# Attention with a soft mixture of experts on one core: filler products in two waits of TensorE, and SyncE's written order kept for eight more weight loads

## The chip, the cores and the metric

The kernel runs on one core of a Trainium2 chip. The metric is the device time of one execution in microseconds, the median of several runs. The profile is one further execution, recorded by the hardware.

## The reference

The first half is attention for 8 batches and 8 heads over 576 positions of width 64: queries and keys are rotated by position, the scores go through a softmax, and the result multiplies the values. The second half sends all 4608 rows of the attention output (512 wide) through a soft mixture of 8 experts with 4 slots each.

```python
q_rot, k_rot = rotate(q), rotate(k)
scores = scale * q_rot @ k_rot.T ; attn = softmax(scores) ; x = attn @ v      # rows: 4608 x 512
logits = x @ phi                                                              # 4608 x 32
d = exp(logits - logits.max(0)) ; d /= d.sum(0)
slot_input = (d.T @ x).reshape(8, 4, 512)
slot_out[e] = relu(slot_input[e] @ w1[e]) @ w2[e]                             # w1 512x1024, w2 1024x512
c = softmax(logits, axis=1) ; out = c @ slot_out
```

## The kernel before

**Attention.** Two heads make a pair, and there are 32 pairs (`NPAIR`), 0 to 31. A pair's products run in units: `m` units find the row maxima of the scores, which ScalarE turns into a small tile `mr` (`m_half`) and SyncE copies by two small DMAs into the rows of a tile `peak` (`m_rows`, lines 340 and 341). The `t` units (line 355, and 368 to 370 for the remainder) form the scores again in three half-precision products and subtract the maxima by a fourth product of `lift` and `peak`; ScalarE takes the exponential (line 358). The `av` units (lines 411 and 422) multiply by the values. Then come `norm`, `natural` (transposes, line 325), `natural_out` (ScalarE copies to `xt`, line 474), `logits` (lines 481 and 484) and `logits_sum`.

**Order.** Three tables of due times, `FIRST`, `WHEN` and `LAST`, sort all steps of all pairs into one list. `tc.manual_schedule` makes an engine issue in the order in which the code is written. For TensorE, ScalarE and VectorE that holds in the whole kernel. For SyncE and GpSimd it holds only while the stack `steady` is open; once it is closed, the framework's scheduler chooses where these two engines' later instructions go, and may put a load ahead of instructions that the code wrote earlier.

**Weights.** The expert weights are 64 tiles of 128x1024 floats (512 KB each), 0 to 31 for the first product and 32 to 63 for the second. Thirty are loaded during attention. The next ones go to room that the last pairs free, and all of them are issued by SyncE from line 612:

- `release_io` (once the last pair's queries and keys are split) opens five buffers `wx`, and `release_stk` opens `wk` (for tile 6), `wh1` and `wh0`. These eight loads are not written at that place but appended to the list `later`, which `trickle` empties.
- `release_fore` opens five buffers `wq` and writes their five loads at once.
- `release_att` opens four buffers `wl` and writes four loads.

The due times put every `trickle` step ahead of `release_io`, so the list is emptied by the loop `while later: trickle(p)` behind the last pair. By the order of the calls, `wq` holds tiles 26 to 30, `wx` 31 and 37 to 40, `wk` 6, `wh1` 41, `wh0` 42, and `wl` 43 to 46.

**Behind the last pair.** `natural`, `logits` and their sum for pair 31, the last statistics (`m_run`), and a chain of small products (lines 821 to 865) that ends in the slot inputs `slot_t`. `spend(n, t)` issues n products of the constant tile `lift` with itself, whose result nobody reads; `SPEND` says how many at each of five places. Then the first expert product runs in four parts `ffn1` (line 889), each with 16 tiles' worth of operands: the first part uses tiles 0 to 7. `ffn2_steps` (line 910) is the second product, in four quarters, and `combine` (line 938) forms the output, copied out by ScalarE and VectorE (line 939) into six buffers and written by 18 DMAs of 512 KB (line 941). Seventeen further loads (tiles 47 to 63) take the buffers that the first product frees. `seg_in` (line 875) is a small load between the two groups of loads.

Of the kernel before, what the change touches and what calls it, by code (L numbers as in the profile page):

```python
# [18 lines left out]
NPAIR = B * NP  # L19
# [22 lines left out]
STAGE = (("wx", 5),) * 5 + (("wh0", 1),)  # L42
LEAD_STEPS = 6
N_SLOT = 1
SPEND = (0, 4, 2, 0, 6)
STEPS = (0, 0, 5, 0, 0, 5, 0, 0, 0)
N_WARM = 17
N_HEAT = 12
# [128 lines left out]
def attn_softmoe(ctx, tc, qk, q0, v, phi, w, cs, ident, sel, seg, out):  # L177
    nc = tc.nc
    P = 128
# [24 lines left out]
    steady = ctx.enter_context(ExitStack())  # L204
# [11 lines left out]
    lift = const.tile([P, P], F16, name="lift")  # L216
# [66 lines left out]
    def bank2():  # L283
        turn_of[0] = (turn_of[0] + 1) % 3
        return slots[turn_of[0]].tile([P, 2, 512], F32, name="s_ps")
# [36 lines left out]
    flat = {}  # L322
# [120 lines left out]
    def recip(p):  # L443
        if p not in ons:
            ons[p] = blocks(o_flat[:, O_AT:O_AT + 2 * NJ * VC])
        rrs[p] = rr = small.tile([P, 2 * NJ, 1], F32, name="rr", bufs=2)
        nc.vector.reciprocal(out=rr, in_=ons[p][:, :, D:VC])  # L447
# [28 lines left out]
    def logits(p):  # L476
        xt = xts.pop(p)
        xj = xt[:, 0:512].rearrange("p (h j x) -> p j h x", h=2, j=4)
        flat["l", p] = lp = bank2()[:, 0]
        for j in range(4):  # L480
            nc.tensor.matmul(lp[32 * j:32 * j + 32, 0:P], lhsT=phi_sb[:, p % NP, :], rhs=xj[:, j],
                             start=True, stop=True, tile_position=(0, 32 * j))
        for j in range(4):
            nc.tensor.matmul(lp[32 * j:32 * j + 32, P:192], lhsT=phi_sb[:, p % NP, :], rhs=xt[:, 512:S],  # L484
                             start=True, stop=True, tile_position=(0, 32 * j))
# [123 lines left out]
    def load_w(pool, bufs, tag="w_exp", n=None):  # L609
        n = order.pop(0) if n is None else n  # L610
        wt = pool.tile([P, 2, 512] if n < 4 * E else [P, 4, 256], F32, name=tag, bufs=bufs)
        nc.sync.dma_start(out=wt, in_=w[n].rearrange("p (c f) -> p c f", c=2 if n < 4 * E else 4))
        w_tiles[n] = wt
# [6 lines left out]
    def grow(name, bufs):  # L620
        hold[name] = ctx.enter_context(tc.tile_pool(name=name, bufs=bufs, side="right", reuse_waits="tile"))
        return hold[name]
# [6 lines left out]
    def trickle(p):  # L629
        if later:  # L630
            name, bufs, n = later.pop(0)
            load_w(hold[name], bufs, n=n)
# [10 lines left out]
    def release_att():  # L643
        trans.close()
        grow("wl", N_WL)
        for _ in range(N_WL):
            load_w(hold["wl"], N_WL)
# [20 lines left out]
    def first_rows(p):  # L668
# [26 lines left out]
        "natural": but_last(natural),  # L695
        "natural_out": but_last(natural_out),
        "logits": but_last(logits),
        "logits_sum": but_last(logits_sum),
        "trickle0": trickle, "trickle1": trickle, "trickle2": trickle, "trickle3": trickle,
# [73 lines left out]
        if "wq" not in hold and not held and all(x in done for x in FORE):  # L773
            release_fore()
    p = NPAIR - 1
    steady.close()
    ac, vc = nc.scalar.copy, nc.vector.tensor_copy
    while later:
        trickle(p)
    release_att()  # L780
    recip(p)
    norm(p, nc.vector, True)
# [2 lines left out]
    c_tr(0)  # L785
    natural_out(p)
    logits(p)
    logits_sum(p)
    stat = stat_tasks(B - 1)
# [26 lines left out]
    def spend(n, t):  # L816
        for _ in range(n):
            nc.tensor.matmul(t[:, 256:384], lhsT=lift, rhs=lift, start=True, stop=True)

    spend(SPEND[0], sp)  # L820
    nc.tensor.transpose(mt[:, 0:P], m.broadcast_to([P, P]), id_sb)
    spend(SPEND[1], sp)
    nc.tensor.transpose(tm[:, 0:P], dt[:, 0:P], id_sb)
    spend(SPEND[2], sp)
    nc.tensor.transpose(tr[:, 0:P], dt[:, D:192], id_sb)
    spend(SPEND[3], sp)
    nc.vector.tensor_copy(out=dn[:, 0:P], in_=tm[:, 0:P])
# [18 lines left out]
    for i in range(NP):  # L846
        nc.tensor.matmul(rp[32 * i:32 * i + 32], lhsT=dn[rows[1], P + 32 * i:P + 32 * i + 32],
                         rhs=xn[i][rows[1], 4], start=True, stop=True, tile_position=(64, 32 * i))
# [18 lines left out]
    nc.vector.reciprocal(out=zw, in_=zw)  # L867
    spend(SPEND[4], mt)
    left.close()
# [169 lines left out]
```

## Time and profile before

| | |
|---|---|
| median of 3 runs | 506.17 us |
| lowest and highest | 503.56 and 509.76 us |
| the profiled execution | 507.91 us |
| its span, first to last instruction | 506.1 us |
| mean granted TensorE clock | 0.990 |
| TensorE busy | 478.3 us, 95% |
| VectorE, ScalarE, GpSimd busy | 72%, 57%, 52% |

The span is what the views below show; the profiled execution took a little longer than its span and than the median. A view of waits tells how long an engine stood idle and what ended that. A view of windows gives busy times, the granted clock and the rate of the DMA engines in stretches of the span.

### The profile page before, as it was taken

To read this page: it belongs to the slowest core of one execution; us is meant where nothing else is said; L and a number is where in the kernel's file an instruction comes from. 1 tells how busy PE (TensorE), PEld (TensorE's weight loads), DVE (VectorE), ACT (ScalarE), POOL (GpSimd) and SP (SyncE) were. 2 spreads that over 40 slices of the span, in tenths; PEclk is the share of its full clock that TensorE was granted. 3 is DMA by queue.
4 is the path that set the end of the run, shared out by engine and by line. 5 is a ranking of instruction groups with operands and counts; after the bars stand their busy time and mean duration, and the time that the engine had idled before them with its cause. 6 is when DMAs were issued, how large, how long until landed. Compare 5 with 4: busy or idle time off the path is not lost. (4 is left out here: it accounts for less than half of the span.)

```text
span 506.1 us, 24787 instructions
## 1 busy us (share of the span) xinstructions
PE 478.3 (95%) x11269; PEld 377.9 (75%) x11269; DVE 362.5 (72%) x497; ACT 290.6 (57%) x522; POOL 265.4 (52%) x330
## 2 busy tenths in 40 slices
PE   4799999999999999999999989999999999899993
PEld 2577778878887888788778867887787886753872
DVE  5879879887788788777788668868887761236453
ACT  2355565675657666766676565765566555424442
POOL 3496697945954576458536845576657201120000
PEclk9999999999999999999999999999999999979998
DMA  7325553343544355434544444355335537579888
GB/s 265 127 96 184 212 188 126 122 166 122 206 164 166 122 191 180 157 126 168 204 123 141 136 179 146 125 190 182 128 139 167 187 100 296 199 272 408 330 349 334
DMA packets 27721, 93.96 MB, mean 186 GB/s; under 512 B 4064, under 2 KB 4320, under 8 KB 27616
## 3 DMA queue, kind: packets, MB, share of 16 engines
q1 hardware_dynamic: 27328, 91.79, 50.5%
q8 instruction: 88, 1.44, 1.1%
q10 hardware_dynamic: 288, 0.59, 0.3%
q14 instruction: 17, 0.14, 0.1%
HBM read 82.85 MB, written 9.44 MB: 182 GB/s over the span
## 5 line engine op out<-in xcount | busy, mean ns | idle before, releaser
L253 POOL TENSOR_TENSOR x_in<-x_in,cs_sb 128x288 f32<-128x288 f32 x248 | 206.1, 869 | 106.7 <-DMA x_in<-in_qk 76.0
L303 DVE TENSOR_REDUCE segs<-s_ps 128x14 f32<-128x896 f32 (+1 forms) x160 | 173.6, 1113 | 52.9 <-PE s_ps L300 48.4
L411 PEld LDWEIGHTS o_ps<-v_in,a_t 128*64 128x64 f32 x4608 | 147.1, 137 | 18.4 <-issue 16.6
L411 PE MATMUL o_ps<-v_in,a_t 128*64 128x65 f32 x4608 | 159.2, 224 | 0.9 <-issue 0.6
L358 ACT ACTIVATE a_t<-s_ps 128x896 f32<-128x896 f32 (+1 forms) x160 | 139.5, 943 | 23.3 <-PE s_ps L355 21.1
L355 PE MATMUL s_ps<-hl 64*128 64x448 f16 (+5 forms) x1536 | 121.6, 283 | 0.9 <-DVE segs L303 0.7
L355 PEld LDWEIGHTS <-hl 64*128 64x128 f16 x1536 | 71.8, 94 | 24.5 <-issue 2.0
L451 POOL TENSOR_TENSOR xn<-o_sb,rr 128x512 f32<-128x512 f32 x31 | 33.3, 1075 | 61.3 <-DVE rr L447 47.8
L355 PE MATMUL s_ps<-peak,lift 64*128 64x128 f16 (+5 forms) x512 | 59.3, 283 | 1.2 <-DMA peak<-mr 1.2
L300 PE MATMUL s_ps<-hl 64*128 64x448 f16 (+5 forms) x512 | 56.4, 286 | 0.6 <-DVE segs L303 0.5
L373 ACT ACTIVATE a_rem<-s_ps 128x640 f32<-128x640 f32 x32 | 22.8, 713 | 54.4 <-PE s_ps L370 54.4
L262 ACT CAST hl<-x_in 128x576 f16<-128x576 f32 x62 | 40.6, 673 | 17.0 <-DVE x_in L257 16.9
L270 DVE TENSOR_TENSOR hl<-x_in,hl 128x1152 f16<-128x1152 f32 x32 | 47.6, 1488 | 1.4 <-ACT hl L262 1.3
L257 DVE TENSOR_TENSOR x_in<-x_in 128x1152 f32<-128x1152 f32 x31 | 46.4, 1497 | 2.7 <-POOL x_in L253 2.7
L474 ACT COPY xt<-s_ps 128x576 f32<-128x576 f32 x32 | 20.4, 637 | 43.6 <-PE s_ps L325 43.6
L355 PEld LDWEIGHTS <-lift 64*128 64x128 f16 x512 | 25.9, 94 | 9.8 <-DMA peak<-mr 1.6
L422 PE MATMUL o_ps<-v_in,a_rem 64*64 64x65 f32 x1152 | 29.3, 223 | 3.0 <-issue 2.9
L300 PEld LDWEIGHTS <-hl 64*128 64x128 f16 x512 | 23.7, 95 | 8.8 <-issue 1.9
L315 DVE TENSOR_REDUCE segs<-s_ps 128x2 f32<-128x576 f32 x32 | 24.1, 754 | 7.7 <-PE s_ps L313 7.4
L422 PEld LDWEIGHTS o_ps<-v_in,a_rem 64*64 64x64 f32 x1152 | 25.2, 134 | 4.7 <-issue 4.6
L437 ACT COPY o_sb<-o_ps 128x585 f32<-128x585 f32 x31 | 20.2, 653 | 10.8 <-PE o_ps L422 5.3
L493 DVE TENSOR_TENSOR l_sb<-s_ps,l_sb 128x192 f32<-128x192 f32 x24 | 8.6, 357 | 22.4 <-PE s_ps L484 22.4
(156 smaller groups left out, 536.2 us busy)
## 6 DMA issues: line engine op xcount, KB each, us to landing
x_in<-in_qk SPq DMA_DIRECT2D x62, 576.0 KB
w_exp<-in_w SPq DMA_DIRECT2D x64, 512.0 KB
v_in<-in_v SPq DMA_DIRECT2D x32, 325.0 KB
out<-w_exp SPq DMA_DIRECT2D x18, 512.0 KB
x_in<-in_q SPq DMA_DIRECT2D x4, 288.0 KB
cs_sb<-in_cs ACTq DMA_DIRECT2D x2, 288.0 KB
peak<-mr SPq DMA_DIRECT2D x32, 2.0 KB
peak<-mr SPq DMA_DIRECT2D x32, 0.2 KB
```

The source lines that it names most:

```text
L253: eng.tensor_tensor(out=x[:, :, c], in0=x[:, :, c], in1=cs_sb[:, h, :, at:at + c.stop - c.start], op=ALU.mult)
L257: nc.vector.tensor_tensor(out=x[:, :, 0], in0=x[:, :, 0], in1=x[:, :, 1], op=ALU.add)
L262: nc.scalar.copy(out=halves[p][:, 1 + t], in_=loaded[p][:, t, 0])
L270: nc.vector.tensor_tensor(out=o, in0=x, in1=i, op=ALU.subtract)
L300: nc.tensor.matmul(s[:, h, at], lhsT=hl[rows[h], QH, P * j:P * j + P], rhs=hl[rows[h], KH, cols], start=True, stop=True)
L303: nc.vector.tensor_reduce(out=segs[p % 2][:, 0:8 * SG].rearrange("p (h c) -> p h c", h=2)[:, :, at:at + n // D], in_=s[:, :, 0:n].rearrang ...
L315: nc.vector.tensor_reduce(out=segs[p % 2][:, 8 * SG:8 * SG + 2], in_=s[:, :, 0:HC], axis=AX.X, op=ALU.max, negate=True)
L355: nc.tensor.matmul(s[:, h, at], lhsT=lhs, rhs=rhs, start=(w == 0 and at.start == 0), stop=(w == 3), skip_group_check=True)
L358: nc.scalar.activation(out=a, in_=s[:, :, 0:n], func=AF.Exp, scale=SCALE)
L411: nc.tensor.matmul(o, lhsT=ats[p, k][:, h, b:b + D], rhs=vts[p][:, 2 * i + h], start=(opening[p, h] == u and c not in begun), stop=(closin ...
L422: nc.tensor.matmul(o, lhsT=rems[p][r, at:at + D], rhs=vts[p][r, 8 + h], start=(opening[p, h] == REM and (h, c) not in begun), stop=(closin ...
L451: eng.tensor_tensor(out=x[:, 0:4].rearrange("p j h d -> p h j d"), in0=o[:, 1:9, 0:D].rearrange("p (h j) d -> p h j d", h=2), in1=rr[:, 1: ...
```

## The change

Ten filler products are put ahead of the logits of pair 30 (`p == NPAIR - 2`), into the unused half of the same tile. `SPEND[0]` goes from 0 to 16: sixteen filler products stand ahead of the transpose of `m_run`. And `steady` is closed behind the loop that empties `later`, not ahead of it, so SyncE issues these eight loads where the code writes them.

```diff
-SPEND = (0, 4, 2, 0, 6)
+SPEND = (16, 4, 2, 0, 6)
+N_IDLE = 10
...
     def logits(p):
         xt = xts.pop(p)
         xj = xt[:, 0:512].rearrange("p (h j x) -> p j h x", h=2, j=4)
-        flat["l", p] = lp = bank2()[:, 0]
+        s = bank2()
+        flat["l", p] = lp = s[:, 0]
+        if p == NPAIR - 2:
+            for _ in range(N_IDLE):
+                nc.tensor.matmul(s[:, 1, 0:P], lhsT=lift, rhs=lift, start=True, stop=True)
...
     p = NPAIR - 1
-    steady.close()
     ac, vc = nc.scalar.copy, nc.vector.tensor_copy
     while later:
         trickle(p)
+    steady.close()
     release_att()
```

SyncE, before, from the first load into `wx` to the first into `wq`, with what each DMA waits for (`DMAHW` are earlier DMAs, the others engines): five loads `wx`, the two copies of pair 31's `peak`, then `wk`, `wh1`, `wh0`, and at the end `wq`, which waits for VectorE, TensorE and GpSimd.

```order
L612 DMA w_exp<-in_w 128x1024 [waits DMAHW3_49,DVE_49,Pool_49]
L612 DMA w_exp<-in_w 128x1024 [waits DMAHW4_49,DVE_49]
L612 DMA w_exp<-in_w 128x1024 [waits DMAHW5_49]
L612 DMA w_exp<-in_w 128x1024 [waits DMAHW6_49]
L612 DMA w_exp<-in_w 128x1024 [waits DMAHW7_49]
L340 DMA peak_115<-mr 2x4x128 [waits DMAHW0_49,Activation_49]
L341 DMA peak_115<-mr 2x1x64 [waits DMAHW1_49]
L612 DMA w_exp<-in_w 128x1024 [waits DMAHW2_49]
L612 DMA w_exp<-in_w 128x1024 [waits DMAHW3_49,PE_49]
L612 DMA w_exp<-in_w 128x1024 [waits DMAHW4_49,PE_49]
L612 DMA w_exp<-in_w 128x1024 [waits DMAHW0_49,DMAHW1_49,DVE_49,DMAHW5_49,PE_49,Pool_49]
```

SyncE, after, from the copies of pair 31's `peak` on: the copies, the five loads `wq`, the five `wx`, and `wk` as the last row.

```order
L341 DMA peak_115<-mr 2x4x128 [waits DMAHW3_49,Activation_49]
L342 DMA peak_115<-mr 2x1x64 [waits DMAHW4_49]
L617 DMA w_exp<-in_w 128x1024 [waits DMAHW3_49,DMAHW4_49,DVE_49,DMAHW5_49,PE_49,Pool_49]
L617 DMA w_exp<-in_w 128x1024 [waits DMAHW6_49]
L617 DMA w_exp<-in_w 128x1024 [waits DMAHW7_49,Activation_49]
L617 DMA w_exp<-in_w 128x1024 [waits DMAHW0_49]
L617 DMA w_exp<-in_w 128x1024 [waits DMAHW1_49]
L617 DMA w_exp<-in_w 128x1024 [waits DMAHW2_49]
L617 DMA w_exp<-in_w 128x1024 x2
L617 DMA w_exp<-in_w 128x1024 [waits DMAHW5_49]
L617 DMA w_exp<-in_w 128x1024 [waits DMAHW6_49]
L617 DMA w_exp<-in_w 128x1024 [waits DMAHW7_49]
```

So all eight loads of `later` have moved behind the two copies of `peak` and behind `wq`; the number of loads is the same.

TensorE, before, from the transposes of pair 30 to the transpose of `m_run`:

```order
L325 MATMUL s_ps<-id_sb,xn 128x64 x9
L481 MATMUL s_ps<-xt,phi_sb 32x128 x4
L484 MATMUL s_ps<-xt,phi_sb 32x64 x4
L325 MATMUL s_ps<-id_sb,xn 128x64 x9
L586 MATMUL o_ps<-id_sb,xn 128x128 x2
L586 MATMUL o_ps<-id_sb,xn 64x128
...
L481 MATMUL s_ps<-xt,phi_sb 32x128 x4
L484 MATMUL s_ps<-xt,phi_sb 32x64 x4
L821 MATMUL t_ps<-id_sb,m_run 128x128
```

TensorE, after, the last of the ten and what stands behind it:

```order
L484 LDWEIGHTS lift
L484 MATMUL s_ps<-lift 128x128
L486 MATMUL s_ps<-xt,phi_sb 32x128 x4
L489 MATMUL s_ps<-xt,phi_sb 32x64 x4
L326 MATMUL s_ps<-id_sb,xn 128x64 x9
...
L823 LDWEIGHTS lift
L823 MATMUL t_ps<-lift 128x128
L826 MATMUL t_ps<-id_sb,m_run 128x128
```

The ten stand between pair 30's transposes and its logits, the sixteen between pair 31's logits and the transpose of `m_run`; nothing else on TensorE has moved, and the orders of ScalarE, VectorE and GpSimd are as before.

## Rows read from the trace of the kernel before

**Rows 1.** The page's first line.
```profile
span 506.1 us, 24787 instructions
```

**Rows 2.** Waits of TensorE from 405 to 500 us: total, times, longest.
```profile
PE t_ps L821 <- DVE m_run L503: 1.2, 1, 1.2
...
PE s_ps L481 <- ACT xt L474: 0.8, 1, 0.8
```

**Rows 3.** Timeline, ScalarE and TensorE, 421 to 429 us: start, us, instruction, [idle before].
```profile
421.35 0.25 ACT L335 ACTIVATE mr<-s_ps 9x128 f16<-9x128 f32 x1
...
427.46 0.36 PE L355 MATMUL s_ps<-peak,lift 64*128 64x448 f16 x2 [1.20 <-DMA peak<-mr]
```

**Rows 4.** Timeline of SyncE's queue, 415 to 478 us.
```profile
415.85 6.13 SPq L612 DMA_DIRECT2D w_exp<-in_w  x5
...
422.67 0.51 SPq L341 DMA_DIRECT2D peak<-mr  x1
423.22 18.37 SPq L612 DMA_DIRECT2D w_exp<-in_w  x12
...
452.82 16.02 SPq L612 DMA_DIRECT2D w_exp<-in_w  x17
```

**Rows 5.** Timeline of the first pair's `peak`: the second copy, and its first user.
```profile
18.97 0.51 SPq L341 DMA_DIRECT2D peak<-mr  x1
...
20.50 0.32 PE L368 MATMUL s_ps<-peak,lift 64*64 64x320 f16 x1 [1.11 <-DMA peak<-mr]
```

**Rows 6.** Windows: length, busy us of each engine, granted clock, DMA share, GB/s.
```profile
423.00:429.00 6.00, 4.80 (x117) 3.67 (x113) 0.00 (x0) 1.70 (x3) 0.00 (x0) 1.00 0.98 382
...
435.00:441.00 6.00, 5.22 (x165) 4.69 (x162) 2.07 (x6) 2.00 (x4) 0.00 (x0) 1.00 0.84 289
...
456.00:475.00 19.00, 19.00 (x286) 10.70 (x282) 9.04 (x19) 7.83 (x18) 0.88 (x1) 1.00 1.02 409
...
494.00:504.00 10.00, 4.24 (x16) 2.40 (x15) 4.31 (x7) 3.70 (x8) 0.00 (x0) 0.96 1.01 402
504.00:506.00 2.00, 0.00 (x0) 0.00 (x0) 0.00 (x0) 0.00 (x0) 0.00 (x0) 0.50 0.13 51
```

**Rows 7.** SyncE's queue: its wait from 424 to 436 us, and loads from 434 us.
```profile
SPq L612 <- PE s_ps L355: 10.4, 1, 10.4
434.44 7.15 SPq L612 DMA_DIRECT2D w_exp<-in_w  x10
```

**Rows 8.** Windows around the fall of the clock.
```profile
445.00:446.00 1.00, 1.00 (x24) 0.67 (x24) 0.81 (x3) 0.05 (x1) 0.55 (x2) 0.60 1.01 410
446.00:452.00 6.00, 6.00 (x42) 3.82 (x38) 1.86 (x7) 0.82 (x2) 2.08 (x3) 0.50 0.70 277
```

**Rows 9.** Timeline of TensorE and its weight loads (PEld), 443 to 459 us.
```profile
443.22 0.34 PEld L818 LDWEIGHTS <-lift 128*128 128x128 f16 x4
443.35 0.39 PE L818 MATMUL t_ps<-lift 128*128 128x128 f16 x4
...
443.82 0.28 PE L818 MATMUL t_ps<-lift 128*128 128x128 f16 x2
...
447.48 1.75 PE L865 MATMUL t_ps<-e_sel,acc 128*128 128x32 f32 x8
449.81 4.71 PE L889 MATMUL a_ps<-w_exp,slot_t 128*32 128x512 f32 x32
454.81 3.64 PE L889 MATMUL a_ps<-w_exp,slot_t 128*32 128x512 f32 x32
```

**Rows 10.** Timeline, 443 to 454 us: VectorE's updates, a weight load, GpSimd's copy of `seg_in`.
```profile
443.19 0.13 PEld L821 LDWEIGHTS t_ps<-id_sb,m_run 128*128 128x128 f32 x1 [1.34 <-issue]
...
445.76 1.45 DVE L842 SCALAR_TENSOR_TENSOR acc<-acc,al,t_ps 128x256 f32<-128x256 f32 x4
...
452.63 0.12 PEld L889 LDWEIGHTS a_ps<-w_exp,slot_t 128*32 128x32 f32 x4 [0.31 <-issue]
...
451.61 0.45 POOL L876 CAST seg_sb<-seg_in 128x320 fp32r<-128x320 f32 x1 [2.73 <-DMA seg_in<-in_seg]
```

## The prediction

> **What bounds the kernel now.** I first asked what TensorE waits for, since it is busy 95% of the span: a microsecond taken from its chain is a microsecond off the end as long as nothing else comes due later. From 405 to 500 us the view of waits shows two waits that end in the statistics part, 1.2 us for `m_run` and 0.8 us for `xt` [rows 2]. The timeline shows a third, of 1.20 us, ahead of the product at 427.46 us, which waits for the DMA of the last pair's `peak` [rows 3]. Elsewhere TensorE runs on without a gap of that size, so those are the three waits that the change can touch.
>
> Next the clock. The windows show a granted clock of 0.60 in 445 to 446 us and 0.50 (1.2 GHz) in 446 to 452 us [rows 8]; before and after it is 1.00 (2.4 GHz). A mean of 0.60 is 0.8 us at half, so the half clock lasts 0.8 + 6 = 6.8 us. It follows the two waits of 0.8 and 1.2 us.
>
> Last the DMA engines, since the change moves loads. From 456 to 475 us they run at 409 GB/s with a share of 1.02, and from 494 to 504 us at 402 [rows 6]: in the tail they are full. The last bytes move in 504 to 506 us, 2 us at 51 GB/s or 0.1 MB, so data ends at about 504.3 us and 1.8 us more pass to the end of the span [rows 1, 6]. I therefore make two sums, one for TensorE's chain and one for the DMA engines, and the later one decides.
>
> **The change part by part.**
>
> *SyncE's order, the gain.* Before, five loads of 512 KB are issued from 415.85 us, over 6.13 us, ahead of the two copies of `peak`; the second copy is issued at 422.67 and TensorE gets it at 427.46, 4.8 us later [rows 3, 4]. The DMA engines have a share of 0.98 from 423 to 429 us [rows 6]: the copy shares them with the loads. For the first pair nothing large was ahead, and there the second copy, issued at 18.97, released a waiting TensorE at 20.50, 1.5 us later [rows 5]. After the change these five loads stand behind the copies. `mr` is ready at 421.35 + 0.25 = 421.60 us [rows 3]. Even if the second copy is issued no earlier than now it lands at 422.67 + 1.5 = 424.2 us, and TensorE wants it at 427.46 - 1.20 = 426.26. The wait goes whole, with 2 us to spare: **-1.2 us** for TensorE and for all that it releases. The bounds are 0 (if a score bank is late instead) and -1.2; I take -1.2, because TensorE has no other wait of note up to 438 us.
>
> *SyncE's order, the price.* Before, seven loads (five, and two of the twelve from 423.22, since ten are issued from 434.44 on) go out ahead of a wait of 10.4 us for the last score products [rows 4, 7]. After, SyncE stands at the first `wq` load, which needs the room of `peak` and so waits for the same products; behind it are queued all eight loads of `later`. From there 17 loads go out where ten did, 7 x 0.524 = 3.67 MB more, or 9.0 us at 409 GB/s. Who waits for that?
>
> Tile 6 first. It is used in the first part of the first expert product, and it is now the 11th load in this row. Before, ten loads and the 0.16 MB of `seg_in` had landed when GpSimd took `seg_in` at 451.61 us [rows 10]; an 11th load instead of `seg_in` is 0.36 MB more, 0.9 us: 452.5 us at the latest. At the earliest, with data from 435.5 us (a microsecond behind the first issue) at 405 GB/s and 1 us to land, 11 x 0.524 / 0.405 = 14.2 us give 450.7. When TensorE wants it depends on the clock, below.
>
> Then the queue as a whole. From the first of these loads to the end it has 34 loads, `seg_in` and 18 outputs: 17.83 + 0.16 + 9.44 = 27.4 MB. If it never runs empty: 435.5 + 27.4 / 0.405 = 503.2 us. If the first six microseconds are as slow as now (289 GB/s from 435 to 441, 1.73 MB [rows 6]): 441 + 25.7 / 0.405 = 504.5. Before it ends at 504.3, with pauses when TensorE had not freed a buffer or formed an output. So this sum stands at -1.1 to +0.2 us, and it too starts 1.2 us earlier, since TensorE's products that free the room come 1.2 us earlier: **-2.3 to -1.0 us**. The second-product tiles 37 to 47 land by about 460 us and are wanted from 468 us on; that cover is wide.
>
> The Trainium skill has a rule against this part: its page "DMA: Bandwidth & Descriptors", section "Specifications", limits one core's traffic with HBM to about 358 GB/s. By it the 27.4 MB would need 76.5 us where my sum has 67.7. The trace does not agree: 409 GB/s stood for 19 us [rows 6].
>
> *The filler products.* Four take 0.39 us and two 0.28 us, so one more is 0.055 us by the products; by their weight loads it is 0.34 / 4 = 0.085 us [rows 9]. Ten: 9 x 0.055 + 0.22 = 0.7 us, or 0.85, in a wait of 0.8. Sixteen: 15 x 0.055 + 0.22 = 1.05 us, or 1.36, in a wait of 1.2. They write banks whose readers are done. Hidden by the waits they cost nothing; the upper bound is 0.05 + 0.15 = **0.2 us**, and I take 0.1. Their use can only be in the clock.
>
> *The clock, if it holds.* The small products from 445.4 us on are then faster. VectorE's four updates end at 445.76 + 1.45 = 447.21 us whatever the clock [rows 10], so the eight products of line 865 can't end before about 448.1: at half clock they take 1.75 us, at full clock about 8 x 0.13 by the weight load of line 821 [rows 9, 10]. The first expert product then starts near 448.5, not at 449.81. Its first part takes 3.64 us at full clock against 4.71 [rows 9]. Without another wait that is 1.3 + 1.1 = 2.4 us, but here tile 6 comes in: it is wanted after half the part's data passes, 448.5 + 1.7 = 450.2 us, and lands at 450.7 to 452.5. The part ends 2.0 us after that, at 452.7 to 454.5, against 449.81 + 4.71 = 454.52 before: 0 to -1.8 us of the 2.4 are left. With -1.2 for `peak` TensorE's chain stands at **-1.2 to -3.0 us**.
>
> *The sum.* The later of the two sums decides: about -1.0 to -2.3 us. I take **-1.7**. The profiled execution would come to 507.91 - 1.7 = 506.2 us; it was 1.7 us above the median of the three runs, and from that median the forecast is 506.17 - 1.7 = **504.5 us**.
>
> **The rivals.**
>
> *The clock falls as before.* For it: the fall comes 2 us behind the second wait, in a stretch of small, thin products that the fillers don't touch, and other fillers already stood in it. Against: the two longest waits just ahead of it are filled. Then tile 6 is wanted only at about 452.6 - 1.1 = 451.5 us (now the third quarter of the part starts at 452.63 [rows 10]) and has landed at 449.5 to 451.3, and what is left is 1.2 - 0.1 = 1.1 us: 505.1 us.
>
> *Slower: the wait for tile 6 lets the clock fall inside the first expert product.* The wait may be 0.5 to 2.3 us; before, the clock fell after waits of 0.8 and 1.2 us. From about 1.2 us on I count it as able to. A half clock of 6.8 us [rows 8] over dense products costs 3.4 us: 504.5 + 3.4 = 507.9 us. For it: the place had no wait before. Against: the products on both sides of it are the densest of the kernel.
>
> *The queue never catches up.* The outputs stand behind 9 us of delayed loads. At 395 GB/s, a little under the 402 of the tail, the 27.4 MB take 1.7 us longer, and the gain is gone: 506.2 us. By the page's limit named above it would be 67.7 + 8.8 us, or 513 us; the rows at 409 leave that little chance.
>
> *The change doesn't do what it says.* The fillers outlast their waits by 0.2 us, the clock falls, and something else (a bank, the values) ends the wait that `peak` ended: 506.4 us.
>
> **How the numbers follow.** Forecast 0.45; the clock falls as before 0.2; slower by tile 6 and the clock 0.15; queue 0.14, of which 0.02 by the page's limit; no effect 0.06. The three runs lie 2.6 below and 3.6 us above their median, so a median can be off by some 2 us. The forecast's best end, 506.17 - 2.3 = 503.9, less that gives 501.5 as the low end; the slower rival gives 508 as the high end. Within 2%, about what a measurement of this kernel can tell from no change (10 us), lies nearly everything: same 0.96, faster 0.02, slower 0.02.
>
> **What would show it right or wrong.** The wait of 1.2 us for `peak` is gone and the unit at 427.46 starts 1.2 us earlier; SyncE issues no load between the copies and about 433 us, and then 17 in a row. The granted clock stays 1.00 from 440 to 455 us. TensorE shows a new wait, of 0.5 to 2.3 us, in the first part of line 889 for a `w_exp` DMA. The DMA share stays near 1 from 436 us to the end, with no pause at 450 to 454 us, and data ends 1 to 2.3 us earlier. I would be wrong if the clock falls at another place, if a later part of the expert products waits for its tiles, or if the copies to the output buffers begin to wait for DMAs.

## The result, and the profile after

The changed kernel took 510.50 us (median of 22 executions, 506.97 to 515.75); the kernel before, on the same chips, 506.37 us (22, 502.74 to 510.96). The ratio is 1.0073, with a 95% interval of 1.0049 to 1.0097: slower by 0.7%, less than the 2% of the three chances, but clearly apart from no change. Ratios, here and below, leave out executions more than 1.5% above the fastest of their kernel; the medians do not. The forecast was 504.5, the range 501.5 to 508.

The profiled execution after took 507.71 us, the third fastest of the 22, so its trace shows what a good execution does and not the median; experiment 1 profiles the kernel a second time. The page's first line:

```profile
span 505.9 us, 24836 instructions
```

The length of the attention phase differs by several microseconds between executions of one kernel. I therefore count from a mark M, the start of ScalarE's last `mr`: 421.35 us before [rows 3], 420.94 after. First the timeline (ScalarE's mark, then TensorE):

```profile
420.94 0.25 ACT L336 ACTIVATE mr<-s_ps 9x128 f16<-9x128 f32 x1
...
425.69 0.35 PE L356 MATMUL s_ps<-peak,lift 64*128 64x448 f16 x2
...
437.07 0.73 PE L484 MATMUL s_ps<-lift 128*128 128x128 f16 x10
...
440.16 1.07 PE L823 MATMUL t_ps<-lift 128*128 128x128 f16 x16
441.44 0.29 PE L826 MATMUL t_ps<-id_sb,m_run 128*128 128x128 f32 x1 [0.21 <-DVE m_run L508]
...
446.51 2.77 PE L894 MATMUL a_ps<-w_exp,slot_t 128*32 128x512 f32 x20
451.95 1.91 PE L894 MATMUL a_ps<-w_exp,slot_t 128*32 128x512 f32 x12 [2.67 <-DMA w_exp<-in_w]
...
454.16 3.64 PE L894 MATMUL a_ps<-w_exp,slot_t 128*32 128x512 f32 x32
```

The product that waited 1.20 us for `peak` [rows 3] starts without a wait, at M + 4.75 instead of M + 6.11. The ten and the sixteen fillers stand where waits of 0.8 and 1.2 us stood [rows 2], and of the second 0.21 us are left. New is the wait of 2.67 us in the middle of the first part of the first expert product: after 20 of its 32 instructions, where tile 6 is first read. SyncE's queue:

```profile
421.21 0.54 SPq L341 DMA_DIRECT2D peak<-mr  x1
421.80 0.50 SPq L342 DMA_DIRECT2D peak<-mr  x1
432.89 16.69 SPq L617 DMA_DIRECT2D w_exp<-in_w  x17
450.69 0.33 SPq L880 DMA_DIRECT2D seg_in<-in_seg  x1
451.97 19.95 SPq L617 DMA_DIRECT2D w_exp<-in_w  x17
477.16 23.31 SPq L946 DMA_DIRECT2D out<-w_exp  x18
```

Nothing is issued from 422.3 to 432.89 us; then come 17 loads, tile 6 the eleventh. The windows (length, busy us of each engine, granted clock, DMA share, GB/s):

```profile
433.00:440.00 7.00, 6.88 (x200) 6.01 (x198) 2.07 (x6) 2.65 (x5) 0.00 (x0) 1.00 0.78 267
440.00:450.00 10.00, 8.65 (x117) 5.04 (x107) 4.22 (x15) 2.32 (x9) 3.09 (x7) 1.00 1.03 403
450.00:454.00 4.00, 2.05 (x14) 0.59 (x14) 0.09 (x1) 0.09 (x1) 0.00 (x0) 1.00 1.02 409
454.00:475.00 21.00, 21.00 (x313) 11.59 (x311) 9.96 (x21) 9.51 (x22) 1.32 (x2) 1.00 1.03 408
...
478.00:484.00 6.00, 6.00 (x139) 4.85 (x138) 3.34 (x7) 2.78 (x7) 0.00 (x0) 1.00 1.03 411
...
503.00:504.00 1.00, 0.00 (x0) 0.00 (x0) 0.00 (x0) 0.00 (x0) 0.00 (x0) 0.50 0.68 266
```

The clock is 1.00 through the stretch where it was 0.50 before [rows 8], and from 440 us on the DMA engines are full, but for a share of 0.87 at 492 to 494 us. Data ends at about 503.7 us.

What both traces give from M on, with the profiled executions of the experiments below (us; "part 2" is the second part of the first expert product):

| kernel | first product starts | wait for tile 6 | part 2 starts | second product starts | span ends |
|---|---|---|---|---|---|
| before | 28.46 | none | 33.46 | 47.25 | 84.75 |
| changed | 25.57 | 2.67 | 33.22 | 47.00 | 84.96 |
| changed, again (1) | 25.57 | 4.35 | 36.54 | 50.33 | 87.79 |
| order alone (2) | 25.58 | 3.41 | 35.93 | 50.52 | 88.10 |
| fillers alone (3) | 26.88, 26.53 | none | 30.82, 30.47 | 44.60, 44.25 | 82.25, 81.64 |
| tile 6 alone late (4) | 26.51 | 2.92 | 34.40 | 48.19 | 85.98 |
| tile 6 seventh (4) | 26.59 | none | 30.53 | 44.31 | 82.09 |
| tile 6 first (5) | 25.58 | none | 29.52 | 43.31 | 84.48 |
| fillers in the wait (6) | 25.58 | 0.38 | 33.64 | 47.43 | 86.04 |

### The profile page after: what moved, and what is told of

It reads as the page before. It is cut to its first block, busy times and chain, and to the rows that moved or that the text cites. A ratio compares the mean times of both kernels' runs of the same rounds, so it can differ in the third digit from the quotient of the medians.

```text
span 505.9 us, 24836 instructions
## 1 busy us (share of the span) xinstructions
PE 477.9 (94%) x11295; PEld 377.5 (75%) x11295; DVE 362.8 (72%) x497; ACT 290.4 (57%) x522; POOL 264.9 (52%) x330
## 5 line engine op out<-in xcount | busy, mean ns | idle before, releaser
L452 POOL TENSOR_TENSOR xn<-o_sb,rr 128x512 f32<-128x512 f32 x31 | 33.3, 1073 | 60.8 <-DVE rr L448 32.7
```

Of the source, the lines that this page charges most:

```text
L452: eng.tensor_tensor(out=x[:, 0:4].rearrange("p j h d -> p h j d"), in0=o[:, 1:9, 0:D].rearrange("p (h j) d -> p h j d", h=2), in1=rr[:, 1: ...
```

## The experiments

Ratios are against the kernel before, run on the same chip; the diffs are against the changed kernel unless said.

**1. The change once more**, unaltered.

> The changed kernel unaltered, for a second profile beside the variants of this group. Theory of tile 6 and the clock: ratio 1.005 to 1.009, and in a profile of 508 us or more the clock is 0.50 for some 6 us behind the wait in the first expert product. Queue theory: the clock is held, and the DMA rate from 455 us on is under 400 GB/s.

510.19 us against 506.34, ratio 1.0076 (1.0044 to 1.0109): the loss repeats. This execution shows its usual size better. TensorE's timeline, then windows:

```profile
447.18 2.77 PE L894 MATMUL a_ps<-w_exp,slot_t 128*32 128x512 f32 x20
454.31 3.30 PE L894 MATMUL a_ps<-w_exp,slot_t 128*32 128x512 f32 x12 [4.35 <-DMA w_exp<-in_w]
458.15 3.64 PE L894 MATMUL a_ps<-w_exp,slot_t 128*32 128x512 f32 x32
```

```profile
433.00:440.00 7.00, 6.88 (x194) 6.07 (x190) 2.07 (x6) 3.00 (x5) 0.00 (x0) 1.00 0.67 238
440.00:450.00 10.00, 9.39 (x123) 5.45 (x121) 4.22 (x15) 2.62 (x10) 3.09 (x7) 1.00 1.03 408
450.00:454.00 4.00, 0.00 (x0) 0.00 (x0) 0.00 (x0) 0.00 (x0) 0.00 (x0) 1.00 1.03 409
454.00:455.00 1.00, 0.69 (x8) 0.33 (x10) 0.00 (x0) 0.00 (x0) 0.00 (x0) 0.84 1.03 410
455.00:458.00 3.00, 3.00 (x14) 0.50 (x6) 0.35 (x1) 0.35 (x1) 0.00 (x0) 0.50 1.02 404
...
478.00:484.00 6.00, 6.00 (x130) 4.45 (x119) 4.27 (x9) 3.26 (x9) 0.00 (x0) 1.00 0.67 265
```

The wait is 1.7 us longer than in the first profile, and behind it the granted clock goes to 0.50 (1.2 GHz) for some 3 us, not the 6 expected: the twelve instructions take 3.30 us instead of 1.91. The second product starts 3.3 us later, the outputs too, and the DMA engines, full at 478 to 484 us in the first profile (1.03), now have room there (0.67): TensorE is late, not the queue. The span ends 2.8 us later from M.

**2 and 3. Each half by itself.** Order alone is the kernel before with `steady.close()` behind the loop; fillers alone puts it back ahead:

```diff
+    steady.close()
     while later:
         trickle(p)
-    steady.close()
```

> SyncE's order of the change, without any of its 26 filler products. Queue theory: 509 to 511 us, ratio 1.006 to 1.010, as with the whole change. Tile-6 theory: the clock falls as before in the statistics part, so tile 6 is wanted about 2.5 us later and its wait is under 1 us: 505 to 507.5 us, ratio about 1.000. Filler theory: 504.5 to 506 us, ratio 0.997 to 0.999, by the 1.2 us of the peak wait.

511.22 us against 508.93, ratio 1.0057 (1.0022 to 1.0092).

> The 26 filler products of the change, with SyncE's order of the kernel before. Queue theory (the change is slower because eight weight loads start late and the DMA queue then never empties): the clock is held or not, nothing is late, 504 to 506.5 us, ratio 0.995 to 1.000. Tile-6 theory (TensorE's new wait for tile 6 in the first expert product, and a fall of the clock behind it): the same, 504 to 506.5 us, no wait for a w_exp DMA. Filler theory (the fillers themselves cost the time, by the clock or by delaying the statistics): 509 to 511 us, ratio about 1.007.

507.95 us, ratio 0.9986 (0.9952 to 1.0019); on another chip:

> The 26 fillers alone, once more beside the variant with three loads ahead: they should give the statistics part its full clock in most executions (1.3 us there and 1.1 us in the first expert product), 0.995 to 0.999. If the clock of the kernel before holds in many executions without them (it held in one profile without fillers): 0.998 to 1.001.

506.69 us against 506.64, ratio 1.0016 (0.9984 to 1.0048). So the loss is the order's, and the fillers change nothing that these runs can tell. The trace of order alone (TensorE's timeline) shows wait and half clock again:

```profile
440.18 0.43 PE L481 MATMUL s_ps<-xt,phi_sb 128*32 128x128 f32 x8 [0.78 <-ACT xt L474]
...
443.70 0.29 PE L821 MATMUL t_ps<-id_sb,m_run 128*128 128x128 f32 x1 [1.21 <-DVE m_run L503]
...
448.78 2.77 PE L889 MATMUL a_ps<-w_exp,slot_t 128*32 128x512 f32 x20
454.96 3.63 PE L889 MATMUL a_ps<-w_exp,slot_t 128*32 128x512 f32 x12 [3.41 <-DMA w_exp<-in_w]
459.13 4.44 PE L889 MATMUL a_ps<-w_exp,slot_t 128*32 128x512 f32 x32
```

It has no fillers in the waits of 0.8 and 1.2 us, and yet its first product starts at M + 25.58, as early as with them: here the clock held up to that product without fillers. So the expectation by tile 6, a wait under 1 us, failed: it had counted on the fall of [rows 8]. The mean granted clocks say of the kernel before itself that this fall doesn't come in each execution. 6.8 us at half and the last 2.9 us of the span too make the 0.990 of its profile; 26 of its 99 executions beside the experiments have 0.993 or more. That is some 7 us at half in all, and the end of the span takes 2.7 us or more of it in every profile, so there is no room for such a fall.

**4. Tile 6 alone.** Seven of the eight loads go out early again. In the row that goes out once SyncE's wait for the last score products ends, the first kernel has tile 6 eleventh, as the change has; the second leaves `release_att` where it is, so that the four `wl` loads come behind tile 6, which is then seventh.

```diff
+        for x in list(later):
+            if x[0] == "wx" or (x[0] != "wk" and ("m_rows", NPAIR - 1) in done):
+                later.remove(x)
+                load_w(hold[x[0]], x[1])
...
+    release_att()          # only in the first kernel
     while later:
         trickle(p)
     steady.close()
-    release_att()          # only in the first kernel
```

> The fillers of the change; SyncE issues five wx loads ahead of the copies of peak and wh1 behind them, as the kernel before, and only the load of tile 6 is late: the 11th behind the wait for the last score products, its place in the change. Theory of tile 6 and the clock: a wait of 2.5 to 4 us in the first expert product, a half clock behind it in many executions, ratio 1.003 to 1.007. Queue theory: only one load is late, the DMA engines pause as before, ratio 0.998 to 1.000.

511.86 us against 506.34, ratio 1.0087 (1.0049 to 1.0125).

> As the variant with only tile 6 late, but its load is the 7th behind the wait (ahead of the four wl loads), not the 11th. If the price of the change is that tile 6 lands after it is wanted: four loads of 1.3 us earlier is 5 us, more than the wait of 2.9 us, so no wait for a w_exp DMA and a ratio of 0.997 to 1.000, against 1.0087 for the 11th place. If tile 6 is not it (the late call of release_att, or chance): 1.005 or more.

505.38 us against 506.64, ratio 0.9995 (0.9965 to 1.0025). TensorE's timeline of the one with tile 6 eleventh:

```profile
448.53 2.77 PE L898 MATMUL a_ps<-w_exp,slot_t 128*32 128x512 f32 x20
454.21 1.91 PE L898 MATMUL a_ps<-w_exp,slot_t 128*32 128x512 f32 x12 [2.92 <-DMA w_exp<-in_w]
```

and of the one with it seventh:

```profile
448.10 3.64 PE L898 MATMUL a_ps<-w_exp,slot_t 128*32 128x512 f32 x32
452.04 3.64 PE L898 MATMUL a_ps<-w_exp,slot_t 128*32 128x512 f32 x32
```

The two differ only in whether tile 6 or the four `wl` loads go first, and that decides between the loss and none. Only one load is late in the first, and the queue theory expected no loss there, so a queue that never empties is not the cause of this loss.

**5. Tile 6 first.** The seven others stay late; tile 6 goes out right behind the copies of `peak`.

```diff
+        if ("m_rows", NPAIR - 1) in done and ("wk", 1, WK) in later:
+            later.remove(("wk", 1, WK))
+            load_w(hold["wk"], 1, n=WK)
```

> The change, but the load of tile 6 is issued right behind the two copies of peak, ahead of the five wq loads; the other seven loads stay late. Queue theory: still 16 loads in a row behind the wait, 508.5 to 510.5 us, ratio 1.004 to 1.008. Tile-6 theory: no wait in the first expert product, 504 to 506.5 us, ratio 0.996 to 1.000. Filler theory: 509 to 511 us.

508.84 us against 508.93, ratio 1.0005 (0.9977 to 1.0033): the loss is gone, but no gain is left. The second product starts 3.9 us earlier than before from M, the span ends 0.3 us earlier. The view of waits of ScalarE and VectorE from 476 us on, and windows, show where that went:

```profile
ACT w_exp L947 <- DMA out<-w_exp: 3.6, 2, 3.3
...
DVE w_exp L947 <- DMA out<-w_exp: 2.9, 1, 2.9
```

```profile
450.00:476.00 26.00, 26.00 (x369) 13.57 (x364) 11.40 (x24) 10.20 (x23) 1.32 (x2) 1.00 1.03 407
476.00:504.00 28.00, 22.26 (x369) 15.42 (x360) 13.57 (x24) 11.48 (x26) 0.00 (x0) 1.00 1.02 407
```

The DMA engines are full for 54 us on end, and the copies to the output buffers wait for earlier outputs to leave. The changed kernel has no such waits in either profile. So in this execution the late loads have a price of their own: its span ends 2.4 us later from M than with tile 6 seventh, where the others go out early. The ratios of the two, 1.0005 and 0.9995, are too close to tell it.

**6. Fillers in the wait for tile 6**, 44 of them behind the first half of the part, to hold the clock and leave the wait.

```diff
+N_WAIT = 44
...
         for i in range(NP):
+            if (grp, f, i) == (0, 0, 2):
+                spend(N_WAIT, mt)
```

> The change, and 44 more filler products (2.4 us) in the first part of the first expert product, just ahead of the quarter that waits for tile 6. If most of the loss is the fall of the clock behind the wait for tile 6: the wait shrinks to under 1.5 us, the clock holds, and the ratio goes from 1.0073 to between 0.999 and 1.003. If the wait by itself or the full queue is the loss: 1.006 to 1.009 as before.

510.06 us, ratio 1.0054 (1.0023 to 1.0084), where the changed kernel on the same chip had 1.0076. The clock is 1.00 from 440 to 460 us. The timeline:

```profile
449.60 2.63 PE L824 MATMUL t_ps<-lift 128*128 128x128 f16 x44
452.16 1.05 PE L897 MATMUL a_ps<-w_exp,slot_t 128*32 128x512 f32 x4
453.60 1.91 PE L897 MATMUL a_ps<-w_exp,slot_t 128*32 128x512 f32 x12 [0.38 <-DMA w_exp<-in_w]
```

The two intervals overlap, so what the half clock adds is not settled; most of the loss stays when the clock holds.

**7. All eight loads right behind the copies of `peak`, or three ahead of them and five behind.**

```diff
+        if "wx" in hold and "ahead" not in hold:          # only in the second
+            hold["ahead"] = [trickle(0) for _ in range(3)]
+        if ("m_rows", NPAIR - 1) in done:
+            while later:
+                trickle(NPAIR - 1)
```

> The change, but the loads of the list are issued as soon as the two copies of the last peak are (five wx, wk, wh1 at once, wh0 and wq behind the last score products): peak first, and no load late. Which tile lies in which late buffer changes, not what is computed. Queue theory and tile-6 theory: no wait for peak, no wait for a w_exp DMA, clock held: 502.5 to 505 us, ratio 0.993 to 0.998. Filler theory: 508 to 510 us, ratio about 1.005.

510.91 us against 508.93, ratio 1.0021 (0.9990 to 1.0051). Its profile has no wait for a weight in the first expert product, and still the gain expected didn't come.

> The fillers of the change, three of the five wx loads ahead of the copies of the last peak, and all others of the list right behind them: tile 6 early, no full queue at the copies. No wait for peak, none for a w_exp DMA, clock held: 0.993 to 0.998. If TensorE's idle times that nothing in the profile ends (3.0 us in the profile of the variant with all loads behind the copies) come with a full DMA queue at 430 to 445 us: shorter here, and the same ratio; if they come at any time: 0.999 to 1.003.

507.24 us against 506.34, ratio 0.9954 (0.9911 to 0.9996). Median and ratio point different ways, so this decides nothing.

> The variant with three wx loads ahead of the copies of peak and the others right behind them, once more, since its first comparison left out many runs (ratio 0.9954, but a median above that of before). If it takes back the wait for peak and the statistics part's half clock and makes nothing late: 0.993 to 0.998. If idle times of TensorE that nothing in the profile ends eat it: 0.999 to 1.002.

505.58 us against 506.64, ratio 0.9989 (0.9961 to 1.0017). No version is shown to beat the kernel before. In all three of these profiles TensorE stands still in the transposes of pair 30, for 2.99, 0.80 and 3.54 us; what that is comes in the last section.

## Why the prediction was wrong

**Right: the waits removed.** The wait for `peak` went whole. I took -1.2 us; from M the product starts 1.36 us earlier. The fillers (0.73 and 1.07 us; I had 0.7 and 1.05) lie in the waits. The first product starts at M + 25.57; the sum, 448.5 less 1.2, made it M + 25.95.

**Failed: when tile 6 lands.** The step "at the earliest ... 1 us to land" to "0.9 us: 452.5 us at the latest", less 1.2, puts it at M + 28.2 to 30.0. Measured, it let TensorE go at M + 31.0 (changed), 32.7 (again), 31.8 (order alone), 32.2 (tile 6 alone late) and 31.4 (fillers in the wait). The wait was 2.7 to 4.4 us, not 0.5 to 2.3.

The rate was not at fault. Tile 6 ends the first 11 loads, 5.77 MB. In the changed kernel 7 us at 267 GB/s and 9.7 at 403 bring that many bytes by 449.7 us; tile 6 landed at 451.95, when 1.87 + 4.03 + 0.80 = 6.70 MB had moved. In the second profile 5.77 MB had moved by 450.0 us, and it landed at 454.31 with 7.5 MB. So 2.3 and 4.3 us lay between, where the prediction had "1 us to land" without a row for it, and meanwhile 0.9 and 1.7 MB of the loads issued behind tile 6 moved.

The trace's records of landings show more. Each of these loads lands in sixteen pieces, and TensorE goes on within 0.05 us of tile 6's last one (us from M):

| kernel | twelve of tile 6's sixteen pieces landed | all sixteen |
|---|---|---|
| changed | 29.7 | 31.0 |
| changed, again | 29.2 | 32.6 |
| order alone | 29.5 | 31.7 |
| tile 6 alone late | 30.3 | 32.1 |
| fillers in the wait | 29.7 | 31.4 |

Twelve pieces came about when the prediction had the whole tile; the last ones came 1.3 to 3.5 us later. That lag is in the row from early on: in the second profile the fourth load's fifteenth piece landed at 441.90 us and its last at 445.32. Nor does it need a row of loads behind: with tile 6 alone late, tile 6 ends its row, and behind it stood only `seg_in` and, from 450.46 us on, loads into freed buffers. Why a few pieces run behind the others is not shown. The prediction also had tile 6 wanted after half of the part, where the trace has 20 of 32 instructions; that alone would have made the wait shorter.

**The rival that came.** The slower rival, a wait for tile 6 that lets the clock fall inside the product, had a chance of 0.15 and 507.9 us, +1.7. The wait came in every profile that issued tile 6 eleventh; the half clock behind it in those with 3.41 and 4.35 us, and not in those with 2.67 and 2.92. The loss is 4.1 and 3.8 us by the medians. From the first profile to the second, 1.7 us more of wait and 1.4 of half clock make nearly all of the 3.3 by which part 2 starts later. How many executions have the half clock can't be told from two profiles of this kernel. The argument against this rival, that dense products stand on both sides, was no protection.

**Failed: the gain by the clock.** I counted 2.4 us for a clock that holds, and set it against a median. It was read from one execution, 1.7 us above that median, in which the clock fell. Order alone held the clock without fillers, and fillers alone are worth nothing in two comparisons (0.9986 and 1.0016), though both profiles end 2.5 to 3.1 us earlier from M than the one of before, in which the clock fell. What one execution lost is no sum for the median unless a second one shows the same loss.

**Failed in part: the queue's sum.** I put the end of data 2.3 to 1.0 us earlier, so at M + 80.7 to 82.0. In the changed kernel's first profile the engines hardly pause from 440 us on, and still data ends at 503.7, M + 82.7; before it was M + 82.9. The seven microseconds at 267 GB/s at the front cost 7 x (403 - 267) / 403 = 2.4 us against a queue that is full at once; the prediction's upper bound had 6 x (405 - 289) / 405 = 1.7 for that. Even with no wait for tile 6 (experiment 5) the queue leaves 0.3 us. The Trainium skill, page "DMA: Bandwidth & Descriptors", section "Specifications", would have it limited to about 358 GB/s; 403 to 411 stood here again, so that limit is not what held it.

## What to carry to other kernels

When loads are put off and then go out in one row, cost the one that is wanted first by when its last piece lands, here 2 to 4 us after the bytes up to it had moved, and give it an early place; that one place, here eleventh or seventh, was worth the whole loss. A stall or a half clock seen in one execution is a sum for that execution; profile the unchanged kernel twice before setting it against a median. Price TensorE and the DMA queue to the end each by itself: in experiment 5, 3.9 us off TensorE's chain left 0.3 us at the end, because the queue was full.

## What the runs showed of the hardware that I had not expected

TensorE can stand still for 3 us and more with nothing in the trace that it waits for by a semaphore. Three ahead, again (TensorE's timeline):

```profile
435.27 0.34 PE L326 MATMUL s_ps<-id_sb,xn 64*128 64x64 f32 x4
439.15 0.59 PE L326 MATMUL s_ps<-id_sb,xn 64*128 64x64 f32 x5 [3.54 <-issue]
```

The kernel with all loads behind the copies has 2.99 us at the same instruction; in both the DMA engines are full there. Three ahead, the first time:

```profile
440.54 0.40 PE L326 MATMUL s_ps<-id_sb,xn 64*128 64x64 f32 x5 [0.80 <-issue]
```

The DMA queues at 436 to 438 us, three ahead, again (queue, packets, MB, share):

```profile
q1 hardware_dynamic: 200, 0.73, 95.6%
q8 instruction: 1, 0.02, 2.8%
```

and the changed kernel at 432 to 434 us, where TensorE does not stop:

```profile
q1 hardware_dynamic: 9, 0.04, 9.5%
q8 instruction: 1, 0.02, 3.2%
```

A packet of the queue named "instruction" moves in the stretch of the long stall and in a stretch without one, beside a nearly full and a nearly empty data queue, so that it moves tells nothing by itself. When it starts does. The packet that comes sixth from M - 13 on starts at M + 12.1 in the changed kernel, where TensorE begins these transposes at M + 15.7 and does not stop. In the three kernels that stop it starts at M + 14.4, 17.3 and 18.0, and each stall ends 2.5 us behind it, at M + 16.9, 19.8 and 20.5.

The same holds in the thirteen profiles as a whole. TensorE has 90 idle times of over 0.25 us that no semaphore ends, and all 90 end 2.2 to 2.6 us after such a packet starts, while a packet comes only every 5.8 us on the mean. So TensorE most likely waits there for instructions that these packets bring. No experiment moved a packet alone, and why it starts later in the three kernels stays open.
